# Turning q on VectorE in 32 by 32 blocks, with q loaded to the partitions that this needs

## The chip, the cores and the metric

One core of a Trainium2 chip. The metric is the device time of one execution in microseconds (us), as the median of several executions. "Before" is the kernel before the change, "changed" the kernel after it.

## The reference

An attention block without softmax, each row normalised, followed by a two-layer block with a squared ReLU. All data is fp32.

```python
# q, k, v: (8 batches, 8 heads, 576 tokens, 64); w_in: (512, 2048); w_out: (2048, 512)
kv  = np.einsum('bhsd,bhse->bhde', k, v)
out = np.einsum('bhsd,bhde->bhse', q, kv)
rms = np.sqrt(np.mean(out * out, axis=-1, keepdims=True) + 1e-06)
x   = (out / rms * g_norm)                 # then (B,H,S,D) -> (4608 tokens, 512)
r   = np.maximum(x @ w_in, 0.0)
y   = (s * (r * r) + b) @ w_out
```

## The kernel before

The 4608 tokens are worked on in 36 chunks of 128 tokens (`c`), four chunks to a unit (`u`, nine units). Nine chunks (`R = 9`) make up a group of two batches. In a unit, TensorE first does 28 products of the first layer (`mm1`) and then 14 of the second (`mm2`). Between the products of `mm2` stand the steps of the attention of the next unit's four chunks: `turn` (transpose q), `product` (q times kv), the normalisation, and `turn_x`. Only parts are shown; cuts are marked.

```python
def load_q(c, queues=(nc.sync, nc.sync)):          # two chunks, two DMAs each
    t = qp.tile([P, 2, H, D], FP32, name="q_sb", tag="q")
    for i in range(2):
        for s, (b, j) in enumerate(halves(c + i)):
            queues[s].dma_start(
                out=t[s * HB : s * HB + HB, i],
                in_=q[b].rearrange("h (p j) d -> p j h d", j=R)[:, j],
            )
        q_in[c + i] = t[:, i]
# ... cut ...
def turn():                                        # TensorE, then a copy out of PSUM
    # ... cut: ps is a PSUM tile ...
    for p in range(NP):                            # NP = 4
        nc.tensor.transpose(ps[:, p, :], q_in[c][:, 2 * p : 2 * p + 2, :], ident)
    st["qT"] = attp.tile([P, NP, P], FP32, name="qT", tag="qT")
    if first:
        nc.vector.tensor_copy(out=st["qT"], in_=ps)
    else:
        nc.scalar.copy(st["qT"], ps)
# ... cut: in mm2 ...
def x5(j):
    product(5, j, st["x", j], False)
    part("r4", j, st["x", j], b2)
    scaled(rows("o2", j)[:, HN:], st["y", j], st["r4", j])     # second half of o2's columns
def y4(j):
    product(4, j, st["y", j], False)
    scaled(rows("o2", j)[:, :HN], st["y", j], st["r2", j])     # first half
    store("o2", j, 4 * u + 2 + j)
# ... cut: the order in mm2; nxt(n) loads one 1 MB tile of second-layer weights on SyncE's queue ...
    lambda: x5(0),
    seq(lambda: x5(1), nxt(6)),                    # nxt(6): the unit's last tile of weights
    lambda: x3(0), lambda: x3(1), lambda: y4(0), lambda: y4(1),
```

Of the kernel before, what the change touches and what calls it, by code (L numbers as in the profile page):

```python
# [8 lines left out]
FP32 = mybir.dt.float32  # L9
# [6 lines left out]
def kernel(  # L16
# [31 lines left out]



    nc = tc.nc
    P = 128
    B, H, S, D = q.shape
    DM = H * D
    DF = moe_w_in.shape[1]
    HB = P // 2
    R = S // HB
    NP = H // 2
    KC = DM // P
    FC = DF // P  # L60
    CH = B // 2 * R
    TB = 2 * P
    U = CH // 4
    NS = FC // 4
    HN = DM // 2
# [4 lines left out]
    qp = ctx.enter_context(tc.tile_pool(name="qp", bufs=2))  # L70
    attp = ctx.enter_context(tc.tile_pool(name="attp", bufs=2))
# [15 lines left out]
    kv_in, q_in, w_raw = {}, {}, {}  # L87

    def load_kv(b, i, pool, queues=(nc.sync, nc.sync), **kw):

        t = pool.tile([P, 4 * R * D], U32, name="kv_sb", **kw)
        kv_in[b, i] = t.bitcast(FP32).rearrange("p (m l j d) -> p m l j d", m=2, l=2, j=R)
        for m, src in enumerate((k, v)):
# [4 lines left out]
                    in_=src[b, h : h + 2].rearrange("h (p j) d -> p h (j d)", j=R),  # L98
                )

    def halves(c):

        g, i = divmod(c, R)
        if i == 4:
            return [(2 * g, R - 1), (2 * g + 1, R - 1)]
        b, i = (2 * g, i) if i < 4 else (2 * g + 1, i - 5)
        return [(b, i), (b, 4 + i)]

    def load_q(c, queues=(nc.sync, nc.sync)):

        t = qp.tile([P, 2, H, D], FP32, name="q_sb", tag="q")
        for i in range(2):
            for s, (b, j) in enumerate(halves(c + i)):
                queues[s].dma_start(
                    out=t[s * HB : s * HB + HB, i],
                    in_=q[b].rearrange("h (p j) d -> p j h d", j=R)[:, j],
                )
            q_in[c + i] = t[:, i]


    wide = moe_w_in.dtype != FP32
# [75 lines left out]
    def sums_w_in(s):  # L197
        ws[s] = wp.tile([P, 3, KH, 2, P], FP32, name=f"ws_{s}")
        a11, a12 = wa[s][:, :KH], wa[s][:, KH:]
        a21, a22 = wb[s][:, :KH], wb[s][:, KH:]  # L200
        s1, s2, s4 = (ws[s][:, i] for i in range(3))

        def s12():
            add(s1, a21, a22)
            sub(s2, s1, a11)

        def s34():
            sub(a21, a11, a21)
            sub(s4, a12, s2)

        return s12, s34
# [48 lines left out]
    ident = const.tile([P, P], FP32, name="ident")  # L260
# [7 lines left out]
    for h in range(H):  # L268
        e = D // KC
        nc.gpsimd.dma_start(  # L270
            out=g_col[h * e : h * e + e, :], in_=g_norm.rearrange("(e c) -> e c", c=KC)
# [46 lines left out]
    def attention(c, first=False):  # L318




        (b, _), (b1, _) = halves(c)
        st = {}

        def turn():
            if first and c == 0:
                ps = ps_a.tile([P, NP, P], FP32, name="qT_ps", tag="x")
            else:
                ps = ps_t.tile([P, NP, P], FP32, name="qT_ps", tag="t")  # L330
            for p in range(NP):
                nc.tensor.transpose(ps[:, p, :], q_in[c][:, 2 * p : 2 * p + 2, :], ident)  # L332
            st["qT"] = attp.tile([P, NP, P], FP32, name="qT", tag="qT")
            if first:
                nc.vector.tensor_copy(out=st["qT"], in_=ps)
            else:
                nc.scalar.copy(st["qT"], ps)

        def product():
            if first:  # L340
                ps = bank_of("att", "xy"[c % 2]).rearrange("p b (m n) -> p (b m) n", m=2)
            else:
                ps = ps_a.tile([P, NP, P], FP32, name="x_ps", tag="x")
            for w in range(4):
                for p in range(NP):
                    nc.tensor.matmul(  # L346
                        ps[32 * p : 32 * p + 32, w, :],
                        lhsT=st["qT"][:, p, 32 * w : 32 * w + 32],
                        rhs=bd_kv[(b if w < 2 else b1) % 2][:, p, :],
                        start=True,  # L350
                        stop=True,
                    )
            st["x"] = ps.rearrange("p c (l d) -> p (c l) d", l=2)
            st["xn"] = attp.tile([P, H, D], FP32, name="xn", tag="xn")
            nc.scalar.activation(st["xn"], st["x"], AF.Square)  # L355
            st["ss"] = attp.tile([P, H], FP32, name="ss", tag="ss")
            nc.vector.reduce_sum(st["ss"], st["xn"], axis=mybir.AxisListType.X)  # L357

        def norm():
            rms = attp.tile([P, H], FP32, name="rms", tag="rms")  # L360
            nc.scalar.activation(rms, st["ss"], AF.Sqrt, bias=eps_col, scale=1.0 / D)
            inv = attp.tile([P, H], FP32, name="inv", tag="inv")
            nc.vector.reciprocal(inv, rms)
            shape = (P, H, KC, D // KC)
            nc.vector.tensor_tensor(  # L365
                out=st["xn"].rearrange("p h d -> p (h d)").rearrange(
                    "p (c h e) -> p h c e", c=KC, h=H
                ),
                in0=st["x"].rearrange("p h (c e) -> p h c e", c=KC),
                in1=inv.unsqueeze(2).unsqueeze(3).to_broadcast(shape),  # L370
                op=ALU.mult,
            )

        def turn_x():
            u, j = divmod(c, 4)
            if j == 0:
                xT[u] = xp.tile([P, KC, 2 * TB], FP32, name="xT", tag="xT")
            to = xT[u][:, :, j * P : j * P + P]
            nc.vector.transpose(
                out=to, in_=st["xn"].rearrange("p h d -> p (h d)").rearrange("p (c x) -> p c x", c=KC)  # L380
            )
            if j % 2 == 1:
                to = xT[u][:, :, j * P - P : j * P + P]
                for i in range(KC):
                    nc.scalar.activation(  # L385
                        to[:, i], to[:, i], AF.Copy, scale=g_col[:, i : i + 1]
                    )

        return turn, product, norm, turn_x
# [144 lines left out]
        nc.sync.dma_start(out=t, in_=w2_dram[ORDER[n]])  # L534
        ring[u, ORDER[n]] = t

    out_v = out.rearrange("(b p j) n -> b p j n", p=HB, j=R)
    G_OF = {1: "a11", 2: "a12", 3: "a12", 4: "a22", 5: "s1", 6: "a11", 7: "a21"}

    def mm2(u):  # L540
        st = {}
# [10 lines left out]
        def scaled(o, ps, other):  # L552
            nc.vector.scalar_tensor_tensor(o, ps, s_col, other, ALU.mult, ALU.add)  # L553

        b1, b2 = b_row[:, :HN], b_row[:, HN:]
# [7 lines left out]
        def rows(name, j):  # L563
            if (name, j) not in st:
                st[name, j] = outp.tile([P, DM], FP32, name=name, tag=name)
            return st[name, j]

        def store(name, j, c):
            for s, (b, jj) in enumerate(halves(c)):
                half = slice(s * HB, s * HB + HB)  # L570
                nc.sync.dma_start(out=out_v[b, :, jj, :], in_=st[name, j][half])

        def half(key, tag, bufs=2):
            return bank_of(key, tag, bufs).rearrange("p b n -> p (b n)")[:, :HN]
# [49 lines left out]
        def x5(j):  # L624
            product(5, j, st["x", j], False)
            part("r4", j, st["x", j], b2)
            scaled(rows("o2", j)[:, HN:], st["y", j], st["r4", j])

        def x3(j):
            product(3, j, st["x", j], False)  # L630
# [3 lines left out]
        def y4(j):  # L634
            product(4, j, st["y", j], False)
            scaled(rows("o2", j)[:, :HN], st["y", j], st["r2", j])
            store("o2", j, 4 * u + 2 + j)

        def seq(fn, *more):
            def run():  # L640
# [114 lines left out]
    turn, product, norm, turn_x = zip(*(attention(c, True) for c in range(4)))  # L755
# [30 lines left out]
    def side_of(u):  # L786

        if u + 1 >= U:
            return {}
        turn, product, norm, turn_x = zip(*(attention(c) for c in range(4 * u + 4, 4 * u + 8)))  # L790
        product = [whole(*steps) for steps in zip(product, norm)]
        side = {
            2: [turn[0]],
            3: [product[0]],
            4: [turn[1]],
            5: [turn_x[0], product[1]],
            6: [turn[2]],
            7: [turn_x[1], product[2]],
            8: [turn[3]],
            9: [turn_x[2], product[3]],  # L800
            11: [turn_x[3]],
            12: [lambda: [sums() for sums in x_sums(u + 1)]],
        }
        if u == 0:
            side = {
                6: [lambda: kv_product(1)],
                7: [turn[0]],
                8: [product[0], turn[1]],
                9: [turn_x[0], product[1], turn[2]],
                10: [turn_x[1], product[2], turn[3]],  # L810
                11: [turn_x[2], product[3]],
                12: [turn_x[3]],
                13: side[12] + [lambda: [sums() for sums in sums_w_in(0)]],
            }
        return side

# [23 lines left out]
    for u in range(U):  # L840
# [24 lines left out]
        second, side = mm2(u), side_of(u)  # L865
# [58 lines left out]
```

## Time and profile before

| | before |
|---|---|
| median time | 987.5 us |
| span of the profiled execution | 986.4 us |
| TensorE busy | 965.1 us |
| VectorE, ScalarE busy | 474.6 us, 208.8 us |

The first fence is the chain of work that ended last, in order of time (start us, us, what), at its end:

```profile
975.16 6.92 PE y_ps L84 x32
982.08 0.02 issue
982.10 0.48 DVE o L553
```

The last product (tile 4 of the weights) begins the moment the one before it ends. VectorE scales its result, and 3.8 us later the stores have landed and the span ends. The second fence is the timeline of SyncE's queue (start us, us, engine, line, operation, what, count) in the same stretch:

```profile
954.47 7.23 SPq L534 DMA_DIRECT2D w_sb<-w  x2
972.25 11.47 SPq L571 DMA_DIRECT2D out_dram<-o  x8
```

The next is TensorE's timeline at the end of the first unit; brackets give the idle time before an entry and what ended it:

```profile
147.30 1.89 PE L84 MATMUL z_ps<-xT,wa 128*128 128x256 f32 x8
150.33 1.97 PE L84 MATMUL x_ps<-xs,ws 128*128 128x256 f32 x8 [1.14 <-DVE ws L186]
```

Here TensorE waits for VectorE's sums of the first weights, `ws`.

### The profile page before, as it was taken

To read this page: it belongs to the slowest core of one execution; us is meant where nothing else is said; L and a number is where in the kernel's file an instruction comes from. 1 tells how busy PE (TensorE), PEld (TensorE's weight loads), DVE (VectorE), ACT (ScalarE), POOL (GpSimd) and SP (SyncE) were. 2 spreads that over 40 slices of the span, in tenths; PEclk is the share of its full clock that TensorE was granted. 3 is DMA by queue.
4 is the path that set the end of the run, shared out by engine and by line. 5 is a ranking of instruction groups with operands and counts; after the bars stand their busy time and mean duration, and the time that the engine had idled before them with its cause. 6 is when DMAs were issued, how large, how long until landed. Compare 5 with 4: busy or idle time off the path is not lost.

```text
span 986.4 us, 15059 instructions
## 1 busy us (share of the span) xinstructions
PE 965.1 (98%) x6514; PEld 836.1 (85%) x6514; DVE 474.6 (48%) x777; ACT 208.8 (21%) x386; POOL 6.7 (1%) x18
## 2 busy tenths in 40 slices
PE   4999999999999999999999999999999999999998
PEld 3788888888888888888888888888888888888887
DVE  2789657453444344534345344533454345444431
ACT  2674131112221211121211212121212111211100
POOL 2000000000000000000000000000000000000000
PEclk9899999999999999999999999999999999999999
DMA  9588728522551355133543255226113330323033
GB/s 231 190 303 249 244 81 230 139 86 97 161 140 50 121 150 118 55 132 77 154 108 127 65 150 140 86 86 172 43 43 129 99 115 3 129 79 132 1 128 85
DMA packets 74225, 121.56 MB, mean 123 GB/s; under 512 B 41776, under 2 KB 47920, under 8 KB 66864
## 3 DMA queue, kind: packets, MB, share of 16 engines
q1 hardware_dynamic: 72208, 119.16, 40.0%
q10 hardware_dynamic: 1632, 1.44, 0.6%
q8 instruction: 51, 0.84, 0.4%
q14 instruction: 14, 0.11, 0.0%
q0 software_dynamic: 320, 0.00, 0.0%
HBM read 103.81 MB, written 16.78 MB: 122 GB/s over the span
## 4 chain that ended last, share of the span: by engine, by line
PE 93%; DVE 3%; DMA 2%; ACT 1%; issue 0%; SPq 0%; ACTq 0%; DVEq 0%
PE x_ps L84 49%; PE y_ps L84 30%; PE z_ps L84 8%; PE x_ps L346 3%; PE kv_ps L299 2%; PE qT_ps L332 1%; DMA kv_sb<-in_v_dram 1%; DMA q_sb<-in_q_dram 1%; DVE ws L186 1%; ACT xT L385 0%; DVE xs L186 0%; DVE ws L183 0%; DVE a L183 0%; SPq L96 0%; DVE xn L365 0%
## 5 line engine op out<-in xcount | busy, mean ns | idle before, releaser
L84 PE MATMUL x_ps<-w_sb,a 128*128 128x256 f32 x768 | 173.6, 381 | 0.0
L84 PEld LDWEIGHTS x_ps<-w_sb,a 128*128 128x128 f32 x768 | 144.2, 190 | 21.5 <-issue 2.8
L84 PE MATMUL y_ps<-w_sb,a 128*128 128x256 f32 x640 | 144.0, 380 | 0.0
L84 PEld LDWEIGHTS y_ps<-w_sb,a 128*128 128x128 f32 x640 | 119.9, 190 | 16.8 <-issue 1.4
L84 PE MATMUL x_ps<-xs,ws 128*128 128x256 f32 x512 | 121.1, 379 | 1.4 <-DVE ws L186 1.1
L84 PE MATMUL y_ps<-xs,wb 128*128 128x256 f32 x512 | 121.0, 379 | 0.0
L481 ACT COPY r<-x_ps 128x512 f32<-128x512 f32 x96 | 56.3, 586 | 298.2 <-PE x_ps L84 290.2
L84 PEld LDWEIGHTS x_ps<-xs,ws 128*128 128x128 f32 x512 | 97.1, 190 | 15.3 <-issue 1.5
L84 PEld LDWEIGHTS y_ps<-xs,wb 128*128 128x128 f32 x512 | 97.3, 190 | 13.2
L183 DVE TENSOR_TENSOR a<-y_ps,r 128x512 f32<-128x512 f32 x64 | 44.0, 687 | 122.1 <-ACT r L481 122.1
L84 PE MATMUL x_ps<-xT,wa 128*128 128x256 f32 x384 | 90.9, 384 | 0.0
L84 PEld LDWEIGHTS x_ps<-xT,wa 128*128 128x128 f32 x384 | 73.9, 193 | 10.6 <-ACT xT L385 0.4
L553 DVE SCALAR_TENSOR_TENSOR or<-x_ps,s_col,b_row 128x256 f32<-128x256 f32 x52 | 25.0, 482 | 92.5 <-PE x_ps L84 88.3
L438 DVE SCALAR_TENSOR_TENSOR a<-a 128x512 f32<-128x512 f32 x96 | 66.4, 692 | 3.3
L84 PE MATMUL x_ps<-xT,ws 128*128 128x256 f32 x256 | 61.1, 381 | 0.0
L84 PE MATMUL z_ps<-xT,wa 128*128 128x256 f32 x256 | 60.5, 379 | 0.0
L514 DVE TENSOR_TENSOR a<-a 128x512 f32<-128x512 f32 x32 | 22.1, 692 | 75.9 <-ACT a L513 75.9
L84 PE MATMUL x_ps<-w_sb,s 128*128 128x256 f32 x256 | 58.5, 382 | 0.0
L84 PEld LDWEIGHTS z_ps<-xT,wa 128*128 128x128 f32 x256 | 48.6, 190 | 6.6
L84 PEld LDWEIGHTS x_ps<-xT,ws 128*128 128x128 f32 x256 | 48.1, 190 | 6.7
L84 PEld LDWEIGHTS x_ps<-w_sb,s 128*128 128x128 f32 x256 | 47.5, 190 | 7.3 <-issue 1.4
L357 DVE TENSOR_REDUCE ss<-xn 128x8 f32<-128x512 f32 x36 | 24.6, 684 | 53.5 <-ACT xn L355 52.7
(93 smaller groups left out, 829.4 us busy)
## 6 DMA issues: line engine op xcount, KB each, us to landing
w_sb<-w SPq DMA_DIRECT2D x56, 1024.0 KB, 5.2
out_dram<-o SPq DMA_DIRECT2D x72, 128.0 KB, 2.3
q_sb<-in_q_dram SPq DMA_DIRECT2D x70, 128.0 KB, 6.0
kv_sb<-in_k_dram SPq DMA_DIRECT2D x30, 288.0 KB, 5.2
kv_sb<-in_v_dram SPq DMA_DIRECT2D x30, 288.0 KB, 6.7
w_raw<-in_moe_w_in_dram SPq DMA_DIRECT2D x8, 1024.0 KB, 6.5
w_raw<-in_moe_w_out_dram SPq DMA_DIRECT2D x8, 1024.0 KB, 5.0
w<-w_up SPq DMA_DIRECT2D x3, 1024.0 KB, 8.1
```

Of the source, the lines that this page charges most:

```text
L84: nc.tensor.matmul(o, lhsT=lhsT, rhs=rhs, start=start, stop=stop, skip_group_check=True)
L183: nc.vector.tensor_tensor(out=o, in0=a, in1=b, op=ALU.add)
L186: nc.vector.tensor_tensor(out=o, in0=a, in1=b, op=ALU.subtract)
L299: nc.tensor.matmul(ps[r][l * HB : l * HB + HB, i, :], lhsT=kv[rows, 0, l, j, :], rhs=kv[rows, 1, l, j, :], start=(j == 0), stop=(j == R - 1),)
L332: nc.tensor.transpose(ps[:, p, :], q_in[c][:, 2 * p : 2 * p + 2, :], ident)
L346: nc.tensor.matmul(ps[32 * p : 32 * p + 32, w, :], lhsT=st["qT"][:, p, 32 * w : 32 * w + 32], rhs=bd_kv[(b if w < 2 else b1) % 2][:, p, :] ...
L357: nc.vector.reduce_sum(st["ss"], st["xn"], axis=mybir.AxisListType.X)
L438: nc.vector.scalar_tensor_tensor(t, t, 0.0, t, ALU.max, ALU.mult)
L481: nc.scalar.copy(st[name], src)
L514: nc.vector.tensor_mul(t, t, t)
L553: nc.vector.scalar_tensor_tensor(o, ps, s_col, other, ALU.mult, ALU.add)
```

## The change

The intent is to take the transposes of q off TensorE. VectorE can turn 32 by 32 blocks from SBUF to SBUF, if the block that is wanted already lies in the right partitions. So for chunks 9 to 35, q is loaded in pieces of 32 partitions and 32 channels: rows of 128 B, with the tokens of a batch laid out as 32 rows of 18 columns (`JC = 18`). The output of these chunks is stored in that order of tokens, in four pieces of 32 rows. Two small things come with it: the last chunk's second half of the columns is stored early and its first half from two queues, and the first sums of weights run one step earlier. The diff is cut to its core:

```diff
+    JC = S // 32
-    def halves(c):
+    def parts(c):                       # (batch, first column, columns); 9 columns before chunk 9
+        n = 1 if g == 0 else 2
+        if i == 4:
+            return [(2 * g, 8 * n, n), (2 * g + 1, 8 * n, n)]
+        return [(b, i, 1), (b, 4 + i, 1)] if g == 0 else [(b, 4 * i, 4)]
 # load_q, chunks from 9 on; pieces are runs of columns of one batch
+        for w, b, j, n in pieces:
+            src = q[b].rearrange("h (t j) d -> h t j d", j=JC)
+            for h in range(H):
+                for a in range(2):
+                    rows = slice(32 * (2 * (h % 2) + a), 32 * (2 * (h % 2) + a) + 32)
+                    nc.sync.dma_start(
+                        out=to[rows, h // 2, w : w + n, :],
+                        in_=src[h, :, j : j + n, a * 32 : a * 32 + 32])
 # turn
+            if c >= R:
+                nc.vector.transpose(out=st["qT"], in_=q_in[c])
+                return
 # store
+            for s, (b, jj) in enumerate((b, jj + i) for b, jj, n in parts(c) for i in range(n)):
+                queues[s % 2].dma_start(
+                    out=view[b, jj, :, cols], in_=st[name, j][s * w : s * w + w, cols])
+        def last(j):
+            return u == U - 1 and j == 1
 # x5
+            if last(j):
+                store("o2", j, 4 * u + 2 + j, slice(HN, DM))
 # y4
+            if last(j):
+                store("o2", j, 4 * u + 2 + j, slice(0, HN), (nc.sync, nc.scalar))
 # end of the first unit
-                12: [turn_x[3]],
-                13: side[12] + [lambda: [sums() for sums in sums_w_in(0)]],
+                12: [turn_x[3], lambda: [sums() for sums in sums_w_in(0)]],
+                13: side[12],
```

More of the change, by code (lines that the diff above doesn't have):

```diff
@@ L99, in load_kv @@
                 )
-    def halves(c):
+    def parts(c):
         g, i = divmod(c, R)
+        n = 1 if g == 0 else 2
         if i == 4:
-            return [(2 * g, R - 1), (2 * g + 1, R - 1)]
+            return [(2 * g, 8 * n, n), (2 * g + 1, 8 * n, n)]
         b, i = (2 * g, i) if i < 4 else (2 * g + 1, i - 5)
-        return [(b, i), (b, 4 + i)]
+        return [(b, i, 1), (b, 4 + i, 1)] if g == 0 else [(b, 4 * i, 4)]
     def load_q(c, queues=(nc.sync, nc.sync)):
-        t = qp.tile([P, 2, H, D], FP32, name="q_sb", tag="q")
+        t = qp.tile([P, 2 * DM], FP32, name="q_sb", tag="q")
+        pieces = []
@@ L112, in load_q @@
         for i in range(2):
-            for s, (b, j) in enumerate(halves(c + i)):
-                queues[s].dma_start(
-                    out=t[s * HB : s * HB + HB, i],
-                    in_=q[b].rearrange("h (p j) d -> p j h d", j=R)[:, j],
-                )
-            q_in[c + i] = t[:, i]
+            if c + i < R:
+                q_in[c + i] = t[:, i * DM : i * DM + DM]
+                to = q_in[c + i].rearrange("p (h d) -> p h d", h=H)
+                for s, (b, j, _) in enumerate(parts(c + i)):
+                    queues[s].dma_start(
+                        out=to[s * HB : s * HB + HB],
+                        in_=q[b].rearrange("h (p j) d -> p j h d", j=R)[:, j],
+                    )
+                continue
@@ new lines, in load_q @@
+            w = 4 * i
+            for b, j, n in parts(c + i):
+                if pieces and pieces[-1][1] == b and pieces[-1][2] + pieces[-1][3] == j:
+                    pieces[-1][3] += n
+                else:
+                    pieces.append([w, b, j, n])
+                w += n
+            q_in[c + i] = t.rearrange("p (a w) -> p a w", a=NP)[:, :, i * P : i * P + P]
+            if c + i == R:
+                q_in[R] = t[:, DM:].rearrange("p (a w) -> p a w", a=NP)
+        for w, b, j, n in pieces:
+            src = q[b].rearrange("h (t j) d -> h t j d", j=JC)
+            to = t.rearrange("p (a w d) -> p a w d", a=NP, d=32)
+            if c < R:
+                to, w = t[:, DM:].rearrange("p (a w d) -> p a w d", a=NP, d=32), 0
+            for h in range(H):
[3 more added lines that the diff above has]
+                        out=to[rows, h // 2, w : w + n, :],
+                        in_=src[h, :, j : j + n, a * 32 : a * 32 + 32],
+                    )
@@ L318, in attention @@
     def attention(c, first=False):
-        (b, _), (b1, _) = halves(c)
+        b, b1 = parts(c)[0][0], parts(c)[-1][0]
         st = {}
         def turn():
-            if first and c == 0:
+            st["qT"] = attp.tile([P, NP, P], FP32, name="qT", tag="qT")
+            if c >= R:
+                nc.vector.transpose(out=st["qT"], in_=q_in[c])
+                return
+            if c == 0:
                 ps = ps_a.tile([P, NP, P], FP32, name="qT_ps", tag="x")
@@ L331, in turn @@
             for p in range(NP):
-                nc.tensor.transpose(ps[:, p, :], q_in[c][:, 2 * p : 2 * p + 2, :], ident)
-            st["qT"] = attp.tile([P, NP, P], FP32, name="qT", tag="qT")
+                nc.tensor.transpose(ps[:, p, :], q_in[c][:, p * P : p * P + P], ident)
             if first:
@@ L535, in load_w2 @@
         ring[u, ORDER[n]] = t
-    out_v = out.rearrange("(b p j) n -> b p j n", p=HB, j=R)
+    out_9 = out.rearrange("(b p j) n -> b j p n", p=HB, j=R)
+    out_18 = out.rearrange("(b t j) n -> b j t n", t=32, j=JC)
     G_OF = {1: "a11", 2: "a12", 3: "a12", 4: "a22", 5: "s1", 6: "a11", 7: "a21"}
@@ L566, in rows, with store @@
             return st[name, j]
-        def store(name, j, c):
-            for s, (b, jj) in enumerate(halves(c)):
-                half = slice(s * HB, s * HB + HB)
-                nc.sync.dma_start(out=out_v[b, :, jj, :], in_=st[name, j][half])
+        def store(name, j, c, cols=slice(0, DM), queues=(nc.sync, nc.sync)):
+            view = out_9 if c < R else out_18
+            w = view.shape[2]
+            for s, (b, jj) in enumerate((b, jj + i) for b, jj, n in parts(c) for i in range(n)):
+                queues[s % 2].dma_start(
+                    out=view[b, jj, :, cols], in_=st[name, j][s * w : s * w + w, cols]
+                )
+        def last(j):
+            return u == U - 1 and j == 1
         def half(key, tag, bufs=2):
@@ L636, in y4 @@
             scaled(rows("o2", j)[:, :HN], st["y", j], st["r2", j])
-            store("o2", j, 4 * u + 2 + j)
+            if last(j):
+                store("o2", j, 4 * u + 2 + j, slice(0, HN), (nc.sync, nc.scalar))
+            else:
+                store("o2", j, 4 * u + 2 + j)
         def seq(fn, *more):
```

## The prediction

> **What bounds the kernel now.** I read the page's busy table first, then the chain of work that ended last, then that chain piece by piece inside one repeating unit, then the waits of the matmul engine, then the groups of the line that turns q.
>
> ```profile
> PE 965.1 (98%) x6514; PEld 836.1 (85%) x6514; DVE 474.6 (48%) x777; ACT 208.8 (21%) x386; POOL 6.7 (1%) x18
> PE 93%; DVE 3%; DMA 2%; ACT 1%; issue 0%; SPq 0%; ACTq 0%; DVEq 0%
> ```
>
> TensorE is busy for 965 of 986.4 us and is 93% of the chain. A busy TensorE alone would not prove a bound, since matmuls overlap and their ends are modelled, so I look for time in which it waits. From 40 us on, its waits are three, 1.8 us together:
>
> ```profile
> PE x_ps L84 <- DVE ws L186: 1.1, 1, 1.1
> PE x_ps L346 <- DVE xn L365: 0.5, 1, 0.5
> PE x_ps L84 <- ACT r L481: 0.2, 1, 0.2
> ```
>
> So the time is the sum of TensorE's instructions, plus about 15 us of start and 4 us of end. Only work taken off TensorE, or one of these gaps, shortens it; VectorE at 48% and ScalarE at 21% have room. What one turn of q costs on that path is read from the chain in order of time, in the third unit (start us, us, what):
>
> ```profile
> 311.10 3.45 PE z_ps L84 x16
> 314.55 0.44 PE qT_ps L332 x4
> 314.99 3.46 PE y_ps L84 x16
> 318.44 1.01 PE x_ps L346 x32
> 319.45 3.65 PE x_ps L84 x16
> 323.10 0.44 PE qT_ps L332 x4
> ```
>
> Four transposes take 0.44 us from the end of one product to the start of the next, and the product behind them keeps its usual 3.45 us: no fixed cost of switching comes with a turn. The 0.2 us extra (3.65) stands behind the attention product (L346), which stays.
>
> **What the Trainium skill says.** "TensorE: Matmul & The Clock Gate", Part 4 (PE-mode transpose), gives about 275 ns for a transpose inside one kernel, and says that the result goes to PSUM and must be copied out. The trace agrees with both: the median transpose record is 273 ns, and each turn is followed by a copy (L337, ScalarE, 584 ns). But 273 ns is latency: four in a row cost the path 0.44 us, or 0.109 us each. The sum needs the second figure. "VectorE: DVE Perf Modes", section "The three transpose paths", says that VectorE turns only 32 by 32 blocks, SBUF to SBUF. The trace has such an operation of just this size, the turn of x (last row below). The blocks must then already lie in the right partitions, hence the new loads. "DMA: Bandwidth & Descriptors", Specifications, names 512 B as the least size for full rate. The trace agrees: around 471 us, rows of 8 KB move at 393 to 426 GB/s with the queues full; at 476 to 478 us, where q's rows of 256 B are left, it is 206 and 179 GB/s. The change halves these to 128 B. The same page, "Issuing engines are not separate DMA queues", says that a second issuing queue saves only issue time, which bears on the last store.
>
> ```profile
> L332 PE MATMUL qT_ps<-ident,q_sb 128*128 128x128 f32 x144 | 23.2, 288 | 1.9 <-DMA q_sb<-in_q_dram 1.9
> L337 ACT COPY qT<-qT_ps 128x512 f32<-128x512 f32 x32 | 18.7, 584 | 105.2 <-PE qT_ps L332 105.2
> L379 DVE STREAM_TRANSPOSE xT<-xn 128x512 f32<-128x512 f32 x36 | 25.2, 702 | 0.2
> ```
>
> **The change, part by part.**
>
> *Turns off TensorE.* There are 36 chunks of 128 tokens; those from 9 on change, 27 of them. The built instruction order confirms it: 27 groups of four transposes are gone from TensorE, 27 block transposes have come to VectorE, and the other products stand in the same order. At 0.435 us a turn (four of 0.109), 27 turns give 11.7 us, all of it on the path because TensorE does not wait there.
>
> *The copy out of PSUM.* 27 x 0.584 = 15.8 us leave ScalarE, which is not on the path in these units: worth nothing by itself.
>
> *Block transposes.* 27 x 0.702 = 19.0 us come to VectorE (48% to some 50%). What matters is each one's place in VectorE's queue. The turn of a unit's first chunk comes right after the scaling of product 2's first half, which in the unit above starts at 314.59 and takes 0.48 us. VectorE then had nothing until 318.48, and the attention product that needs the result starts at 318.37. The transpose should be done near 315.8, some 2 us ahead. The second falls behind the normalisation of the first chunk and is ready near 324.4 for a product at 326.9; the third and fourth find VectorE idle for longer. No new wait of TensorE is expected, and the normalisation itself moves by at most one 0.7 us step.
>
> *Loads of q.* In the later groups, the 2 loads of 128 KB a chunk become 16 small ones for a run of tokens: 32 to 64 issues a unit in place of 8, and 8192 rows of 128 B in place of 4096 of 256 B. The old ones took 0.66 us each to issue (median). If the new ones take the same, the worst unit needs 64 x 0.66 = 42 us of the queue. As to moving: 256 B rows went at about 200 GB/s, so one engine of the 16 handles a row in about 256 B x 16 / 200 GB/s = 20 ns; if a half row costs no less, 8192 rows take 8192 x 20 / 16 = 10 us, and at twice that 20 us. Issue decides, not movement. The need comes late: q for the next unit is asked for at the unit's start (467.7 us in the unit that begins at 464.9) and first used after the first phase of 28 products and two more, about 58 us later. The weights of the second phase (third tile) are queued behind q and kv, and move from about 30 us into the unit to some 45; they are used 66 us in. Both hold with about 15 us to spare, so: zero on the path.
>
> *Stores.* Four rows-of-32 stores a chunk in place of two of 64: 8 more issues a unit at 0.55 us, 4.4 us of a queue that waits most of the time. Zero.
>
> *The last store.* After the last VectorE instruction (482 ns, ending at 982.58) come two issues, then 256 KB, landing 2.3 us after issue, then the close at 986.4. Now half the columns have gone ahead, so 128 KB are left, in four stores from two queues, two each as before. At some 200 GB/s the 128 KB saved are 0.6 us; I take 0.5.
>
> *The sums of the first weights* run one step earlier at the end of the first unit. There TensorE waited 1.14 us for them and then 0.24 us for an evicting copy held up by the same full VectorE stretch (145.8 to 166 us). Four sums of 0.6 us each leave that stretch, more than the wait: I take 1.2 us.
>
> Sum: 11.7 + 1.2 + 0.5 = 13.4 us, so 987.5 - 13.4 = 974.1 us, 1.4% less.
>
> **The rivals.** *(1) The loads become the bound.* If an issue of q took 1 us or more, or 128 B rows cost several times a 256 B row, the worst unit (64 issues) would need over 58 us, and the first transposes or the third weight tile would come late. Against it: q's issue times (0.60 us minimum, 0.66 median) are much the same as kv's (0.61) although kv has far fewer, longer rows; rows do not seem to set them. For it: a few old q issues took 2.3 to 5.5 us when the queue behind them was full. At 1.2 us an issue, only the unit with 64 would surely stall, by some 20 us: about 990 us in all. One chance in twenty. *(2) The transpose is late on VectorE*, so that a wait for VectorE takes the place of the transposes. The margins above are about 2 us each; if half of the 27 lost 0.5 us, some 6 us would be given back: 980 us. The places of the other instructions speak against it. *(3) Only the latency was in the page:* if one believed the 273 ns records, 108 transposes would give 29 us and 958 us. The chain speaks against it.
>
> **Range and chances.** The main term is read directly and repeats in all units, so I trust it within 0.3 us; the two small terms are uncertain by some 0.7 us; run to run spread is 0.8 us. A margin upwards is for small waits of rival 2. Range 972.6 to 977.0. Two per cent would need 967.8 us, which only a cause that I do not see could give: 2%. Slower by 2% needs rival 1 in a bad form: 3%. The rest, 95%, is within 2%.
>
> **What would show it.** TensorE should have 108 instructions fewer and 11 to 12 us less busy; a full unit of four turned chunks should last 104.0 us in place of 105.74; waits of TensorE after 40 us should be under 1 us; the block transpose should read near 700 ns; q's small issues near 0.6 us; and from the last VectorE instruction to the close about 3.3 us in place of 3.8. A wait of the attention product for the turned q, a wait of a product for weights, or issues of q above 1 us would make the prediction wrong.

## The result, and the profile after

The changed kernel takes 974.7 us (median of 4, 974.58 to 975.02) against 987.53 us: 12.8 us less. The ratio is 0.9871, with a 95% interval of 0.9854 to 0.9888. Here and below a ratio is from the fast runs of the same rounds; it is not quite the quotient of the medians quoted. The prediction of 974.1 us, 972.6 to 977.0, holds the time.

The page's busy table of the changed kernel:

```profile
PE 951.6 (98%) x6406; PEld 824.5 (85%) x6406; DVE 490.1 (50%) x804; ACT 193.4 (20%) x359; POOL 6.7 (1%) x18
```

108 instructions have left TensorE and 27 have come to VectorE. TensorE's busy time is 13.5 us less, where 11 to 12 were forecast: 11.6 us of this lie in the late stretch of the table below, which holds the turns, and 1.5 us in the start, which the change does not touch. The third unit again, in the chain in order of time:

```profile
306.82 3.45 PE z_ps L87 x16
310.27 3.45 PE y_ps L87 x16
313.73 1.01 PE x_ps L382 x32
314.74 7.11 PE x_ps L87 x32
```

The products follow each other with no turn between them, and the next unit's z product starts at 410.80: 103.98 us a unit, where it was 105.74. VectorE does the turns at the expected pace (groups by shape: busy us, mean ns, then idle time before):

```profile
L362 DVE STREAM_TRANSPOSE qT<-q_sb 128x512 f32<-128x512 f32 x27 | 18.9, 701 | 0.0
```

The wait for the sums of weights is gone; the product that had to wait now follows at once (TensorE's timeline):

```profile
146.23 1.89 PE L87 MATMUL z_ps<-xT,wa 128*128 128x256 f32 x8
147.95 1.89 PE L87 MATMUL x_ps<-xs,ws 128*128 128x256 f32 x8
```

But the waits of TensorE after 40 us are not all gone. One is new:

```profile
PE y_ps L87 <- DMA w_sb<-w: 1.3, 1, 1.3
PE x_ps L382 <- DVE xn L401: 0.5, 1, 0.5
```

The chain in order of time shows where it is, at the very end, and the timeline of SyncE's queue what stands ahead of the load:

```profile
956.32 5.23 DMA w_sb<-w
961.55 0.04 issue
961.59 7.19 PE y_ps L87 x32
968.78 0.03 issue
968.81 0.48 DVE o L590
```

```profile
954.50 1.73 SPq L609 DMA_DIRECT2D out_dram<-o  x4
956.32 0.37 SPq L570 DMA_DIRECT2D w_sb<-w  x1
```

The early store of the last chunk (`x5`) is queued on SyncE before `nxt(6)`, the last load of weights. The queue works in order. The store waits for VectorE's result until 954.50, and the four issues take 1.73 us, so the load leaves only at 956.32 and lands at 961.55. (How early it could leave is seen in e4.) TensorE has waited 1.26 us for it, and the product behind the wait takes 7.19 us in place of 6.92.

To see where 12.8 us come from, I cut each trace at three marks that all kernels share: the start of the first product into the z tile in the first unit, the start of the same product in the second unit, and the start of the last VectorE instruction. The numbers are differences of start times from the timelines.

| stretch, us | before | changed | difference |
|---|---|---|---|
| start, to z of the first unit | 100.65 | 99.51 | -1.1 |
| middle, to z of the second unit (holds the sums of weights) | 104.54 | 102.72 | -1.82 |
| late, to the last VectorE instruction (holds the 27 turns) | 776.91 | 766.58 | -10.33 |
| end, to the end of the span | 4.30 | 3.89 | -0.41 |

No edit touches the work before the first mark, so the first row is not the change's doing: in the other traces below, this stretch lies between 99.0 and 101.9 us whatever the kernel. That is why the stretches tell small parts better than the times do. That the start also makes the times of one kernel differ by 1 to 3 us is likely, but not shown: the two traces of the changed kernel (this one and e8) have the same start.

### The profile page after: what moved, and what is told of

It reads as the page before. It is cut to its first block, busy times and chain, and to the rows that moved or that the text cites. A ratio compares the mean times of both kernels' runs of the same rounds, so it can differ in the third digit from the quotient of the medians.

```text
span 972.7 us, 15160 instructions
## 1 busy us (share of the span) xinstructions
PE 951.6 (98%) x6406; PEld 824.5 (85%) x6406; DVE 490.1 (50%) x804; ACT 193.4 (20%) x359; POOL 6.7 (1%) x18
## 4 chain that ended last, share of the span: by engine, by line
PE 95%; DMA 2%; DVE 1%; ACT 1%; SPq 0%; issue 0%; ACTq 0%; DVEq 0%
PE x_ps L87 50%; PE y_ps L87 31%; PE z_ps L87 9%; PE x_ps L382 3%; PE kv_ps L331 2%; DMA kv_sb<-in_v_dram 1%; DMA w_sb<-w 1%; PE qT_ps L369 0%; DVE xn L401 0%; ACT xT L421 0%; DVE ss L393 0%; SPq L99 0%; SPq L609 0%; ACT xn L391 0%; DVE o L590 0%
## 5 line engine op out<-in xcount | busy, mean ns | idle before, releaser
L391 ACT ACTIVATE xn<-x_ps 128x512 f32<-128x512 f32 x34 | 20.3, 597 | 192.9 <-PE x_ps L382 190.9
```

Of the source, the lines that this page charges most:

```text
L391: nc.scalar.activation(st["xn"], st["x"], AF.Square)
```

## The experiments

Theory: the turns give 0.44 us each, the sums some 1.8, the end 0.4, and the early store costs 1.5 by its place in the queue. The main rivals: the parts can't be told apart, the new wait comes from the small loads or from chance, or the turns on VectorE and the loads only just fit.

### e1: the turns and loads alone

The sums and the last chunk's store are put back.

```diff
         def last(j):
-            return u == U - 1 and j == 1
+            return False
-                12: [turn_x[3], lambda: [sums() for sums in sums_w_in(0)]],
-                13: side[12],
+                12: [turn_x[3]],
+                13: side[12] + [lambda: [sums() for sums in sums_w_in(0)]],
```

> The kernel before with only the new loads, the block transposes on VectorE and the stores that follow from them; the sums of the first weights are back in their old place and the last chunk is stored as before. Theory (turns are worth 0.435 us each on the path, 27 of them, nothing else of the load change matters): 11.7 us less than before, about 975.8 us; a full unit lasts 104.0 us; the old wait of 1.1 us for the sums of weights is back; the new wait for the last tile of weights (1.3 us in the changed kernel) is absent or far smaller. Rival (the three parts are not separable, the turns gave less and the sums and the store gave the rest): 9 us less or under.

Measured: 975.7 us against 987.5, ratio 0.9880 (0.9865 to 0.9895). The late stretch is 765.04 us, 11.87 less than before: 0.440 us a turn. The middle is 104.55 us, as before. The wait for the sums is back and the wait for weights is absent. This line is from TensorE's waits:

```profile
PE x_ps L87 <- DVE ws L218: 1.1, 1, 1.1
```

So the turns alone give the main part, and the changed kernel's late stretch (766.58) is 1.54 us longer than it need be.

### e2: the sums alone

The kernel before, with the two lines of the sums as in the change.

```diff
-                12: [turn_x[3]],
-                13: side[12] + [lambda: [sums() for sums in sums_w_in(0)]],
+                12: [turn_x[3], lambda: [sums() for sums in sums_w_in(0)]],
+                13: side[12],
```

> The kernel before with only the sums of the first weights moved one step earlier. Prediction on record: 1.2 us less (986.3). Theory after reading both traces: 1.9 us less (985.6), because the wait of 1.1 us, its restart and the wait of 0.2 us for an evicting copy all go; no wait of TensorE for sums of weights is left. Rival (the 1.9 us came from the start of the execution, which varies): under 0.5 us.

Measured: 985.67 us against 987.5, ratio 0.9977 (0.9965 to 0.9990). The middle stretch is 102.80 us, 1.74 less than before; the late one is unchanged to the hundredth (776.91). The rival is out: the gain does not come from the start.

### e3: the last store alone

The kernel before, with its last chunk stored as in the change (two pieces of 64 rows here, not four of 32).

```diff
+            if last(j):                                  # in x5
+                store("o2", j, 4 * u + 2 + j, slice(HN, DM))
-            store("o2", j, 4 * u + 2 + j)                # in y4
+            if last(j):
+                store("o2", j, 4 * u + 2 + j, slice(0, HN), (nc.sync, nc.scalar))
+            else:
+                store("o2", j, 4 * u + 2 + j)
```

> The kernel before with only the last chunk's store changed: its second half of the columns goes out early, on the SyncE queue, ahead of the last load of weights; the first half at the end from two queues. Theory (queue order: the last load of weights stands behind a store that waits for VectorE): a new wait of TensorE for weights, 0.5 to 1.5 us (two early stores here, four in the changed kernel), against 0.4 us less at the end: 0 to 1 us slower than before, 987.5 to 988.5. Rival (the new wait came from the small loads of q, or is chance): no such wait here, and 0.4 to 0.5 us less than before, 987.1.

Measured: 987.98 us against 987.5, ratio 1.0004 (0.9991 to 1.0017), which alone decides nothing. The trace does: the wait for weights is there without any small load of q (TensorE's timeline):

```profile
974.50 7.17 PE L84 MATMUL y_ps<-w_sb,a 128*128 128x256 f32 x32 [0.85 <-DMA w_sb<-w]
```

The late stretch is 1.11 us longer than before, the end 0.52 shorter (3.78). So this part of the change, meant as a gain, loses 0.6 us by itself here.

### e4: the early stores on ScalarE's queue

```diff
             if last(j):
-                store("o2", j, 4 * u + 2 + j, slice(HN, DM))
+                store("o2", j, 4 * u + 2 + j, slice(HN, DM), (nc.scalar, nc.scalar))
```

> The changed kernel with the four early stores of the last chunk issued from ScalarE's queue in place of SyncE's. Theory (queue order): the wait for the last tile of weights goes, 1.5 us less than the changed kernel, about 973.2 us. Rival (the stores' data and the load of weights contend for the DMA engines): the wait stays, at 0.5 us or more, since the stores move at the same time as before; time within 0.5 us of the changed kernel, 974.7.

Measured: 973.02 us against 987.5, ratio 0.9851 (0.9837 to 0.9864). The late stretch is 765.05 us, the same as e1's, and the end 3.89. TensorE's timeline has no gap before the last product:

```profile
953.59 7.07 PE L87 MATMUL x_ps<-w_sb,a 128*128 128x256 f32 x32
960.50 7.07 PE L87 MATMUL y_ps<-w_sb,a 128*128 128x256 f32 x32
```

SyncE's queue shows when the last load of weights leaves if no store stands ahead of it (the second of these two issues starts at 946.9):

```profile
939.98 7.23 SPq L570 DMA_DIRECT2D w_sb<-w  x2
```

It lands 4.7 us later, 8.9 us before the last product needs it. Counted from the start of the product before the last (953.59 here, 953.26 in the changed kernel), the changed kernel's load leaves 9.76 us later than this: 7.94 us because the store waits for VectorE, 1.82 us for the four issues. It also lands 0.5 us more slowly (5.2 us, where e4 has 4.7 and e1 5.0), so contention of the DMA engines, the rival, is at most these 0.5 us. The queue's order is the main cause, but neither the wait for VectorE nor the issues alone would have used up the 8.9 us; together, with the slower landing, they are 1.4 us too long.

### e5: the late turns twice on TensorE

```diff
-                nc.tensor.transpose(ps[:, p, :], q_in[c][:, 2 * p : 2 * p + 2, :], ident)
+                for _ in range(2 if c >= R else 1):
+                    nc.tensor.transpose(ps[:, p, :], q_in[c][:, 2 * p : 2 * p + 2, :], ident)
```

> The kernel before with each late turn of q done twice by TensorE (27 groups of eight transposes in place of four, same result). Theory (a turn costs the path 0.435 us): 11.7 us more than before, 999.2 us. Rival (it costs its latency, 0.27 us a transpose): 29 us more, 1017 us. A second rival (the turn partly hides in a gap, so that its removal gives less than its doubling costs, or the reverse): gain and cost differ by more than 1 us.

Measured: 999.3 us against 987.06, ratio 1.0127 (1.0110 to 1.0144). The late stretch is 788.70 us, 11.79 more: 0.437 us a turn, as the removal gave 0.440. A turn in the chain, where before it was 0.44 us for four:

```profile
314.99 0.87 PE qT_ps L333 x8
323.98 0.87 PE qT_ps L333 x8
```

The latency of 273 ns is not what the path pays, and the third rival of the prediction is out.

### e6: the block transposes twice on VectorE

```diff
-                nc.vector.transpose(out=st["qT"], in_=q_in[c])
+                for _ in range(2):
+                    nc.vector.transpose(out=st["qT"], in_=q_in[c])
```

> The changed kernel with each block transpose on VectorE done twice (19 us more of VectorE's work, same result). Theory (VectorE has over 1 us to spare at each place): 974.7 us as the changed kernel, within 0.5 us, and no new wait of TensorE for VectorE. Rival (a late transpose is just avoided and the margin is thin): a wait of TensorE for the turned q or for the normalised x, and 2 to 10 us more.

Measured: 975.37 us (975.1 to 977.0), ratio 0.9887 to before (0.9873 to 0.9902). The late stretch is 766.53 us against the changed kernel's 766.58, with no new wait of TensorE for VectorE. VectorE's timeline in the third unit:

```profile
311.27 1.45 DVE L363 STREAM_TRANSPOSE qT<-q_sb 128x512 f32<-128x512 f32 x2
314.32 0.48 DVE L591 SCALAR_TENSOR_TENSOR o<-y_ps,s_col,or 128x256 f32<-128x256 f32 x1 [1.60 <-PE y_ps L87]
```

Even two in a row are followed by 1.6 us of idle time. So every turn has at least 0.7 us to spare.

### e7: each small load of q split in two

```diff
-                    nc.sync.dma_start(
-                        out=to[rows, h // 2, w : w + n, :],
-                        in_=src[h, :, j : j + n, a * 32 : a * 32 + 32])
+                    for k in (0, n // 2):
+                        nc.sync.dma_start(
+                            out=to[rows, h // 2, w + k : w + k + n // 2, :],
+                            in_=src[h, :, j + k : j + k + n // 2, a * 32 : a * 32 + 32])
```

> The changed kernel with each small load of q split in two (half the tokens each): the same rows of 128 B, twice the issues, 64 to 128 a unit. At the 0.44 us that an issue took in the changed kernel, the unit with 128 needs some 60 us with its waits, and the third tile of weights, queued behind, then comes 0 to 15 us late; the units with 96 need some 45 us and stay within their slack. Theory (the issue time is per DMA, so the load queue is the next limit): 974.7 plus 3 to 15 us, with one long wait of TensorE for weights in the fifth unit. Rival (issue time follows the rows, so halves take half): no wait, 974.7 us.

Measured: 1015.14 us (1011.19 to 1021.32) against 987.06, ratio 1.0293 (1.0253 to 1.0332). It is 40 us above the changed kernel, where 3 to 15 were expected. SyncE's queue in the fifth unit, and TensorE's timeline there:

```profile
474.84 67.29 SPq L148 DMA_DIRECT2D q_sb<-in_q_dram  x128
547.49 28.57 SPq L571 DMA_DIRECT2D w_sb<-w  x5
```

```profile
536.10 1.08 PE L383 MATMUL x_ps<-bd_kv,qT 128*32 128x128 f32 x32
557.49 10.10 PE L87 MATMUL x_ps<-w_sb,a 128*128 128x256 f32 x32 [20.31 <-DMA w_sb<-w]
```

128 issues take 67.3 us, 0.53 us each with their waits (median of an issue 0.43 us); in the changed kernel 64 took 36.6 us, 0.57 us each (median 0.44 us). Half the rows do not halve the time. The third tile of weights is queued behind them and comes 20.3 us late. The theory's mechanism holds; its size was off for three reasons that the trace shows. The units with 96 issues wait too, some 6 us each, so that these three waits are 32.4 us. The load of weights itself takes 10 us to land. And a product that follows a wait runs slowly, 10.10 us in place of 7.17, since the granted clock falls to 0.50 in the gap and stays there until some 563 us. (The Trainium skill, "TensorE: Matmul & The Clock Gate", Part 1, describes this halving after an idle window of about 3.4 us. The trace agrees with the halving; in its four gaps the clock falls some 2.4 to 4.8 us after the last product's end, so the length of the window is not confirmed.) The three slow restarts add 7.7 us. A fourth wait, of 2.6 us, is in the second unit at 215.40, with 1.6 us for its slow product (8.77 us). The list of waits puts it down to a VectorE instruction (L394), but in the changed kernel the same product starts before that instruction; the third tile of weights, issued at 204.14 behind 64 issues of q, landed 11.1 us later, so it is the likely cause here too. Waits and restarts are 44.3 of the 44.75 us by which the late stretch (811.33 us) is longer than the changed kernel's. The profiled execution is the slowest of the four.

### e8, e9, e10: the changed kernel and two corrections side by side

e8 is the changed kernel, unaltered. e9 keeps the early stores on SyncE's queue but places them behind the load; e10 is e4 again.

```diff
-            seq(lambda: x5(1), nxt(6)),
+            seq(lambda: x5(1), nxt(6), lambda: early(1)),     # e9; early(1): the store taken out of x5
```

> The changed kernel itself, unaltered, so that the two corrected versions can be compared with it on one chip in the same rounds. 974.7 us within 0.5 us; a wait of TensorE of 1.2 to 1.7 us for the last tile of weights is in the trace again (if it is chance, it is absent).

> The changed kernel with the four early stores still on SyncE's queue, but placed behind the last load of weights. Theory (queue order alone): no wait for weights, 973.1 us, as with the stores on ScalarE's queue, and 1.6 us less than the changed kernel. Rival (a store and the load at the same time are what costs, or SyncE's queue is too full at the end): 974 us or more.

> The changed kernel with the early stores on ScalarE's queue, once more, beside the two others: 973.1 us within 0.4 us, 1.6 us less than the changed kernel; no wait of TensorE for weights.

| | median, us | lowest to highest | ratio to before (95%) | start | late | end |
|---|---|---|---|---|---|---|
| e8 changed | 974.80 | 974.00 to 976.38 | 0.9875 (0.9858 to 0.9891) | 99.51 | 766.69 | 3.84 |
| e9 store behind | 974.77 | 972.44 to 975.57 | 0.9868 (0.9853 to 0.9882) | 101.93 | 765.05 | 3.86 |
| e10 store on ScalarE | 973.97 | 972.68 to 975.92 | 0.9865 (0.9849 to 0.9881) | 99.24 | 765.05 | 3.90 |

Before took 987.37 us in these rounds. The wait for weights is in e8's trace again (1.4 us) and in neither of the others; both have the same late stretch, 1.64 us less than e8's. In the times, e9's expected 1.6 us is not seen, and e10's is half seen: with four runs each the intervals overlap, and the start alone differs by 2.7 us between these three profiled executions. So the gain of a correction is shown in the stretch and not by these medians. The version of e4 and e10 has the lowest ratios to before, 0.9851 and 0.9865 in two sets of rounds, but e9's 0.9868 is not clear of them.

## Why the prediction was right

The time lies in the range, the change is within 2%, and the main step was right too. Two of its smaller steps were off in opposite directions, the sums by 0.6 us and the early store by 1.5 us. That the total is within 0.6 us is in part luck, since these two partly cancel.

- **Turns: right.** 11.7 us were predicted, 11.87 us are gone with the turns alone (e1), and 11.79 us come when they are doubled (e5). The unit lasts 103.98 us; 104.0 was predicted.
- **Nothing else of the turns matters: right.** VectorE's block transposes take 701 ns and cause no wait; e6 shows the margin. ScalarE's freed copies are worth nothing: its idle time grew, and the sum needs no term for them.
- **Loads: right, with less to spare than it said.** The small loads took 0.44 us (median) to issue, against 0.6 expected. Still, in the fifth unit q's 64 issues with their waits took from 460.4 to 497.0 us, and the third tile of weights was issued at 502.3, 45 us into the unit, as worked out. It takes up to 10.0 us to land, which the prediction did not count, and is first used at 522.6: 10 us to spare, not 15. e7 shows that beyond this the loads do become the bound.
- **Sums: mis-sized.** 1.2 us were taken, 1.82 measured (1.74 alone, e2). The two waits in the list, 1.14 and 0.24 us, are counted from the modelled end of the product before. From start to start of the products they cost 1.31 and 0.41 us, and the two products behind the waits were 0.17 us slow: 1.9 us in all.
- **"Stores. ... Zero", and "half the columns have gone ahead" in "The last store": this step failed.** I counted how long the stores take on the queue and what is left at the end, and not what stands behind the store that goes ahead. It waits for VectorE at the head of an ordered queue, with the last load of weights behind it. That costs 1.54 us (changed against e1), shown by e3, e4 and e9. It is also why the waits after 40 us are 1.8 us and not "under 1 us". The prediction named a wait of a product for weights as a sign of being wrong; that sign came (1.3 us), but from this store and not from the loads of q that rival 1 had in mind.
- **The last store: about right.** 0.5 us were taken, 0.41 measured: from the end of the last VectorE instruction to the close it is 3.4 us, where 3.3 were forecast. Together with the step above, this part of the change is a loss of 1.1 us.

By the stretches, 11.87 + 1.82 + 0.41 - 1.54 = 12.6 us, against 12.8 in the medians and 13.4 in the prediction. The rest is within what the start varies among the traces.

## What to carry to other kernels

Where one engine never waits, taking work from it gives what that work costs between its neighbours in the chain of work, not what its records last: here 0.44 us for four transposes whose records are 273 ns each. Work that goes to other engines and queues is then free as long as it fits, and it is worth knowing by how much it fits, since past that point it costs its waits and a slow restart of TensorE as well. A transfer moved earlier on an ordered queue delays whatever was behind it: before moving one, look at which load comes next in that queue and when it is needed.

## What the Trainium skill lacked or had wrong

- "DMA: Bandwidth & Descriptors", Issuing engines are not separate DMA queues: it says that a second issuing queue saves only issue time. In e4 it saved more: without the four stores ahead of it on SyncE, the last load of weights left 9.8 us earlier, and only 1.8 us of these were issues; 7.9 us were the store's wait for VectorE. TensorE gained 1.53 us (late stretch 766.58 us changed, 765.05 in e4).
- The same page has no issue time by shape for loads from SyncE that I found. The runs show medians of 0.66 us for 512 rows of 256 B, 0.44 us over loads of 64 to 256 rows of 128 B, 0.33 us for 128 rows of 8 KB, and 0.43 us (0.53 with waits) where half-size loads were queued 128 in a row.
- "TensorE: Matmul & The Clock Gate", Part 4, gives a transpose's duration only. In a row between other products, four fp32 transposes cost the path 0.435 to 0.440 us, 0.11 us each, by removal (e1) and by doubling (e5).
